# S4 block on one core: block-diagonal first transform of the token tiles, and a new order for the front of the program

## The chip, the cores and the metric

The kernel runs on one core of a Trainium2 chip. A core has five engines with in-order instruction streams: TensorE (PE, matrix products into PSUM banks; its weight loads are listed as PEld), VectorE (DVE), ScalarE (ACT, functions with a scale and a bias, and copies), GpSimd (POOL), and SyncE (SP), which here issues nearly all DMA transfers. The metric is the device time of one execution in microseconds (us), as the median of several runs. For one further execution there is a profile: busy times, the order of instructions, and what each waited for. L412 is line 412 of the kernel.

## The reference

The input `u` has 2048 tokens of 640 channels; a condition vector `c` gives six vectors of 640 values (shift, scale and gate, twice).

```python
mod = (silu(c) @ w_mod).reshape(1, 6, 1, 640)      # sa, ca, ga, sb, cb, gb
h = layernorm(x) * (1 + ca) + sa
x = x + ga * A(h)          # A: for each channel a convolution over all 2048 tokens
h = layernorm(x) * (1 + cb) + sb
x = x + gb * ((silu(h @ w1) * (h @ w3)) @ w2)      # 640 -> 1728 -> 640
```

In `A`, the kernel of the convolution of channel d is `K[d, l] = Re sum_n C[d,n] dt[d] B[d,n] exp(dt[d] A[d,n] l)` with 128 values of n, and the product of the spectra (`rfft`, `irfft`) computes the causal convolution; a skip term `h * Dskip` is added. All is float32.

## The kernel before

**Stages.** The convolution runs as small DFT products on PE in two steps, 32 by 64 (NA = 32, NB = 64). The token tiles are j = 0 to 15, each of 128 tokens. The *front* (0 to 163.5 us) loads and prepares all that is needed: it makes polar forms and logarithms of the parameters (`polar`), the modulation vectors, the normalized tiles (`ln1_norm`), the first transform of each tile (`u_stage1`), and for steps s = 0, 1, 2, ... of 16 channels the tables of exponentials and trigonometric values (`exps`, and the parts named PH, AB, CO, SI, E1, E2, A1, A2), from which PE sums the convolution kernels (kg, pt, uk). Then *rounds* follow, one chapter of 128 channels per 54.7 us, in an order that a table writes out (ROUND): second transforms (`stage2`, L571), product of spectra, inverse transforms, and the tables of later steps. The feed-forward network follows from about 410 us to the end.

**What sets the order.** The program is written as calls in sequence. A scheduler may move instructions on PE, DVE, POOL and SP as far as dependencies and buffers let it, but the helpers `act` (L135) and `acopy` (L138) keep all of ACT's instructions in the order in which they are written. PSUM tiles are named by tags (Z, A, B, pb, pk); a tag with one buffer means that a new user waits until the last one has been read.

**Modulation.** Columns of `w_mod` are multiplied by silu(c), spread over four column groups of the array of 32 each. `mod_sums` (L305) gives the blocks k = 0 to 3 to the four groups and block 4 to group 0 again; a one-column matmul (L316 or L358) adds the four groups up. `mod_early` fills `cols`, five of its passes before the first tiles; `mod_cols` makes later ones from weights that `w_load` (L206) brings, near the end of the front. `mod_shift` (L322 to L341) divides shift by scale: the result r is wanted as a row (`pr`, then `rrow`) and, weighted by the column sums of the DFT matrix (c1), as a shift to be added to the transform (`rc`, `ps`, `shift`).

**First transform.** `u_stage1(j)` makes for the four 32-token blocks of a tile the real and imaginary part of a 32-point DFT. Eight matmuls (L412) use 32 rows and 64 columns of the array each, so that eight of them fit beside each other; `pu[0]` (tag Z) takes blocks 0 and 1, `pu[1]` (tag A or B by turns) blocks 2 and 3. For even j four 1-row matmuls (L404) put the shift into `pu[0]` ahead of them, and ACT copies `pu[0]` (L138). For odd j DVE adds the shift while it evacuates `pu[0]` (L417). DVE evacuates `pu[1]` for all j (L418). One DMA of 640 KB (L419) then stores the tile's result to `us` in DRAM; chapters read it back with `u_load` (L557).

**The loop of the front.** For tk = 0, 1, 2, ... the loop makes the tables of step tk + 2, the kernels of earlier steps, the tiles 2 tk + 4 and 2 tk + 5 (the first four stand ahead of the loop), the loads of later x tiles (`ln1_load`, L374, seven buffers) and the normalization of the pair tk + 3 (DVE statistics L383 and L384, POOL L385 and L386, DVE L387, then two ACT instructions x<-x,rs on L135). At tk = 4 to 8 `w_load` is issued, at 5 to 8 `mod_cols(tk - 5)`, at 7 the eight loads of `u_load` for chapter 0, and `mod_cols(4)` stands ahead of the first rounds.

Of the kernel before, what the change touches and what calls it, by code (L numbers as in the profile page):

```python
# [9 lines left out]
F32 = mybir.dt.float32  # L10
# [7 lines left out]
P = 128  # L18
# [19 lines left out]
def consts():  # L38
# [34 lines left out]
    c1 = s1r.reshape(4, NA, 2 * NA).sum(axis=1, keepdims=True).repeat(NA, axis=1).reshape(P, 2 * NA)  # L73
# [5 lines left out]
    misc = np.concatenate([selx, stepx, s1r, c1, one4, toq, tog], axis=1)  # L79
    f = lambda v: np.ascontiguousarray(v, dtype=np.float32)  # L80
    return {"s1": f(s1), "s2": f(s2), "i1": f(i1), "i2": f(i2), "iota": iota, "misc": f(misc),
# [26 lines left out]
def tile_kernel(ctx: ExitStack, tc: tile.TileContext, a):  # L108
# [4 lines left out]
    us = dram.tile([2, 2, NA, NB, D // 2], F32, name="us")  # L113
# [70 lines left out]
    rrow = pm_.tile([P, D], F32, name="rrow")  # L184
    shift = pm_.tile([P, D // 2], F32, name="shift")
    cols = pm_.tile([P, 7, KD], F32, name="cols")
    lt = pm_.tile([P, 2, D - DC], F32, name="lt")
    misc = pm_.tile([P, 9 * NA + 1 + P], F32, name="misc")
    selx, stepx = misc[:, :NA], misc[:, NA:4 * NA]
    s1r, c1, one4 = misc[:, 4 * NA:6 * NA], misc[:, 6 * NA:8 * NA], misc[:, 8 * NA:8 * NA + 1]  # L190
    toq, tog = misc[:, 8 * NA + 1:8 * NA + 1 + P], misc[:, 8 * NA + 1 + P:]
# [7 lines left out]
    l2 = flat[2][:, 4 * D:4 * D + 2 * (D - DC)]  # L199

# [27 lines left out]
    prma = a["prm"].rearrange("i n d -> n i d")  # L228
    nc.sync.dma_start(cT, a["c"])
# [9 lines left out]
    def polar(cs, E):  # L239

        are, aim, br, bi, cr, ci = (prm[:, i, cs] for i in range(6))
        ld, dtc, m, t, g_r, g_i = (v[:, cs] for v in (ldt, dt, m0, t3, gr, gi))
        k0, nk = cs.start // P, (cs.stop - cs.start) // P

        E.tensor_tensor(g_r, br, cr, op=OP.mult)
        E.tensor_tensor(m, bi, ci, op=OP.mult)
        E.tensor_tensor(g_r, g_r, m, op=OP.subtract)
        V.tensor_tensor(g_i, br, ci, op=OP.mult)
        V.tensor_tensor(t, bi, cr, op=OP.mult)
        V.tensor_tensor(g_i, g_i, t, op=OP.add)  # L250
        q, q2, ag, ai = br, bi, cr, ci
        act(q, g_r, AF.Square)
        act(q2, g_i, AF.Square)
        act(ag, g_r, AF.Abs)
        act(ai, g_i, AF.Abs)
        yield
        V.scalar_tensor_tensor(q, q, 1e-36, q2, op0=OP.max, op1=OP.add)
        act(q, q, AF.Ln)

        V.tensor_tensor(m, ag, ai, op=OP.subtract)  # L260
        V.scalar_tensor_tensor(t, ag, 1e-30, ai, op0=OP.max, op1=OP.add)
        V.reciprocal(q2, t)
        V.tensor_tensor(m, m, q2, op=OP.mult)
        act_set("trig_and_small")
        act(m, m, AF.Arctan)
        act(ag, g_r, AF.Sign, scale=-1.0)
        act(ai, g_i, AF.Sign, scale=-1.0, bias=tiny)

        V.scalar_tensor_tensor(aim, aim, 0.25 / math.pi, dtc, op0=OP.mult, op1=OP.mult)
        magic = 12582912.0  # L270
        V.tensor_scalar(t, aim, magic, None, op0=OP.add)
        V.tensor_scalar(t, t, -magic, None, op0=OP.add)
        V.tensor_tensor(aim, aim, t, op=OP.subtract)
        V.tensor_scalar(thi[:, cs], aim, TURN, 2147483520.0, op0=OP.mult, op1=OP.min)
        yield

        nt = 2 * nk
        nat = lambda v: v.rearrange("n (t p r j) -> n t r p j", t=nt, p=4, r=2)
        rows = lambda v: v[:, :nk * P].rearrange("n (t r p j) -> n t r p j", t=nt, p=4, r=2)
        for k in range(nt):  # L280
            E.tensor_tensor(rows(lt[:, 0])[:, k], nat(are)[:, k], nat(dtc)[:, k], op=OP.mult)
        for k in range(nt):
            V.tensor_tensor(rows(lt[:, 1])[:, k], nat(q)[:, k], nat(ld)[:, k], op=OP.add)
        for i, dst in enumerate((la, lm)):
            raw = lt[:, i, :nk * P].rearrange("n (b c) -> n b c", c=32)
            both = l2[:, :2 * nk * P].rearrange("n (b s c) -> n b s c", s=2, c=32)
            acopy(both.bitcast(F32R)[:, :, 0], raw)
            V.tensor_tensor(both[:, :, 1], raw, both[:, :, 0], op=OP.subtract)
            pT = psS.tile([P, 2, 512], F32, name="pT", tag="AB"[i], bufs=1).rearrange("p a b -> p (a b)")
            for k in range(nt):  # L290
                PE.transpose(pT[:, k * P:(k + 1) * P], l2[:, k * P:(k + 1) * P], ident)
            acopy(dst[:, 2 * k0:2 * k0 + nt], pT[:, :nt * P].rearrange("p (k n) -> p k n", k=nt))

        V.tensor_scalar(m, m, 0.5 / math.pi, 0.125, op0=OP.mult, op1=OP.add)
        V.tensor_tensor(m, m, ag, op=OP.mult)
        V.scalar_tensor_tensor(m, m, 0.25, ai, op0=OP.add, op1=OP.mult)
        V.tensor_scalar(phi[:, cs], m, TURN, 2147483520.0, op0=OP.mult, op1=OP.min)  # L297


    def mod_sums(w, pm):  # L300

        n = w.shape[2]
        for k in range(KD):
            g = slice(k % 4 * NA, k % 4 * NA + NA)
            PE.matmul(pm[g, :n], scb[:, k], w[:, k, :], start=(k < 4), stop=(k > 0), tile_position=(0, g.start))  # L305
# [13 lines left out]
    def mod_shift():  # L319
# [9 lines left out]
        for k in range(KD):  # L329
            PE.matmul(pr[:64, k * P:(k + 1) * P], r[:, k:k + 1].broadcast_to([P, 64]), ident, start=True, stop=True)  # L330
        V.tensor_copy(rrow[:64], pr[:64, :D])
        rc = pm_.tile([P, WC], F32, name="part", bufs=2)[:, :KD * 2 * NA].rearrange("p (k c) -> p k c", k=KD)
        V.tensor_tensor(rc, bc(c1, 1, KD), bc(r, 2, 2 * NA), op=OP.mult)
        ps = psS.tile([P, 512], F32, name="ps", tag="pk", bufs=1)
        for k in range(KD):
            for hh in range(2):
                lo, hi = max(k * P, hh * 320), min(k * P + P, hh * 320 + 320)
                if lo < hi:
                    PE.matmul(ps[hh * 64:hh * 64 + 64, lo - hh * 320:hi - hh * 320], rc[:, k],
                              ident[:, lo - k * P:hi - k * P], start=True, stop=True, tile_position=(0, hh * 64))  # L340
        V.tensor_copy(shift, ps[:, :320])  # L341
# [50 lines left out]
    usw = us.rearrange("h c f b d -> (h c f) b d")  # L392
    usr = us.rearrange("h c f b d -> h c b f d")

    def u_stage1(j):
# [3 lines left out]
        u = hpz.tile([P, 4, D // 2], F32, name="u", bufs=2)  # L399
        pu = [psS.tile([P, 2, 512], F32, name="pu", tag=t, bufs=1) for t in ("Z", "AB"[j % 2])]  # L400
        one = j % 2 == 0
        for q in range(2 if one else 0):
            for hh in range(2):
                PE.matmul(pu[0][hh * 64:hh * 64 + 64, q, :320], c1[q * NA:q * NA + 1],  # L404
                          rrow[q * NA:q * NA + 1, hh * 320:hh * 320 + 320],
                          start=True, stop=False, tile_position=(q * NA, hh * 64))
# [1123 lines left out]
```

## Time and profile before

| | |
|---|---|
| median of 3 runs | 968.77 us (967.21 to 969.94) |
| profiled execution | 975.08 us, its span 973.3 us |
| front | 0 to 163.5 us |
| rounds, then the rest of the convolution | 163.5 to about 410 us |
| feed-forward network | about 410 to 973.3 us |
| PE busy over the span | 896.1 us (92%) |
| DVE, ACT, POOL busy | 714.1, 543.0, 282.4 us |

In a row of a timeline stand the start and the length in us, the engine, the line, the operation, output<-inputs by the program's names, sizes, and how many instructions (x) the row joins; in brackets the idle time of the engine before it and what ended that. `PE 32*64 32x320 f32` is a matmul that uses 32 rows and 64 columns of the array and streams 320 columns; a float32 product leaves two records. Tiles that share memory by turns are named after the memory's first user: `uk` or `A` may be a weight block or a parameter. In a row of windows stand the stretch, its length, each engine's busy time with the number of instructions, the clock granted to PE (1.00 is full), the busy share of the DMA engines and GB/s. A row of waits has total, times and longest.

### The profile page before, as it was taken

How to read it: one execution, taken by the hardware profiler on the slowest of the kernel's cores; microseconds unless marked ns; L12 is line 12 of the kernel's file. 1: busy time of each engine (PE TensorE's matmuls, PEld its weight loads, DVE VectorE, ACT ScalarE, POOL GpSimd, SP SyncE). 2: the span in 40 equal slices, each digit the busy share in tenths (PEclk: the TensorE clock that was granted, in tenths of full speed). 3: DMA queues.
4: the chain of work that ended last, by engine and by line, in shares of the span. 5: the costliest groups of instructions: out<-in, count | busy, mean ns of one | idle time of the engine just before them, and what ended most of it. 6: DMA issues, size and time to landing. Idle time of an engine off the chain costs nothing.

```text
span 973.3 us, 20145 instructions
## 1 busy us (share of the span) xinstructions
PE 896.1 (92%) x7984; PEld 675.4 (69%) x7984; DVE 714.1 (73%) x1259; ACT 543.0 (56%) x795; POOL 282.4 (29%) x278
## 2 busy tenths in 40 slices
PE   4978787889888899899999999999999999999998
PEld 2534444666666666567888888777888888888886
DVE  5598865999999996767666665677786766654675
ACT  4568675999999984236433333455743333333332
POOL 1372343455455641113422220121252222200000
PEclk8555777999999999899999999999999999999999
DMA  9463576655665688785213112895422221113443
GB/s 267 143 228 131 198 202 179 163 147 140 170 162 145 171 224 245 220 216 194 91 55 108 55 55 78 234 272 187 146 84 64 77 66 53 54 41 94 149 150 122
DMA packets 103571, 140.73 MB, mean 145 GB/s; under 512 B 20564, under 2 KB 62676, under 8 KB 103476
## 3 DMA queue, kind: packets, MB, share of 16 engines
q1 hardware_dynamic: 99668, 129.34, 46.0%
q0 software_dynamic: 2304, 7.74, 2.4%
q10 hardware_dynamic: 1504, 2.36, 0.8%
q8 instruction: 63, 1.03, 0.4%
q14 instruction: 32, 0.26, 0.1%
HBM read 107.94 MB, written 31.46 MB: 143 GB/s over the span
## 4 chain that ended last, share of the span: by engine, by line
PE 76%; ACT 9%; DVE 7%; DMA 4%; issue 3%; POOL 0%; ACTq 0%; SPq 0%; DVEq 0%; POOLq 0%
PE ps L102 55%; PE p L571 6%; ACT A L135 3%; PE pz L613 3%; PE pk L522 2%; PE pt L540 2%; ACT cs L135 2%; DMA zs<-zt 2%; PE pq L445 2%; PE pa L435 1%; PE pm L305 1%; PE pu L412 1%; ACT uk L138 1%; DMA uk<-in_w_mod_dram 1%; PE pm L316 1%
## 5 line engine op out<-in xcount | busy, mean ns | idle before, releaser
L102 DVE TENSOR_TENSOR s<-ps,s 128x512 f32<-128x512 f32 x138 | 94.9, 688 | 80.4 <-PE ps L102 79.5
L473 POOL TENSOR_TENSOR ph<-thi,iota 128x1024 int32<-128x1024 int32 x40 | 91.9, 2298 | 154.4 <-DVE A L505 54.0
L102 DVE TENSOR_TENSOR gl<-rw,gh 128x640 fp32r<-128x640 f32 x87 | 78.2, 899 | 65.2 <-ACT gh L102 65.1
L102 ACT CAST gh<-rw 128x640 fp32r<-128x640 f32 x87 | 63.3, 727 | 104.2 <-PE ps L102 63.4
L571 PE MATMUL p<-uk,s 128*64 128x256 f32 x640 | 79.4, 390 | 14.0 <-ACT uk L138 5.8
L102 PE MATMUL ps<-xA,gh 128*128 128x512 f32 x280 | 87.8, 392 | 0.4 <-ACT xA L102 0.4
L102 PE MATMUL ps<-gh,uh 128*128 128x512 f32 x224 | 87.5, 391 | 0.0
L102 PE MATMUL ps<-gl,uh 128*128 128x512 f32 x224 | 87.2, 389 | 0.0
L102 POOL TENSOR_TENSOR S<-rw 128x256 f32<-128x256 f32 x46 | 36.8, 801 | 170.7 <-DVE S0l L102 160.0
L102 PE MATMUL ps<-gh,ul 128*128 128x512 f32 x208 | 81.1, 390 | 0.0
L571 PEld LDWEIGHTS p<-uk,s 128*64 128x64 f32 x640 | 45.9, 139 | 37.8 <-issue 9.7
L498 DVE TENSOR_TENSOR E<-A,cs 128x1024 f32<-128x1024 f32 x40 | 60.4, 1511 | 3.2 <-ACT cs L135 2.5
L102 PEld LDWEIGHTS ps<-xA,gh 128*128 128x128 f32 x280 | 52.1, 188 | 13.0 <-ACT xA L102 0.9
L102 PE MATMUL ps<-xA,gl 128*128 128x512 f32 x140 | 54.6, 390 | 0.0
L474 POOL TENSOR_TENSOR ph<-ph,phi 128x512 int32<-128x512 int32 x40 | 48.5, 1213 | 5.0 <-DVE phi L297 2.0
L540 PE MATMUL pt<-s,K 128*64 128x128 f32 x640 | 48.3, 291 | 1.4 <-ACT uk L138 1.4
L505 DVE TENSOR_TENSOR A<-A,ph 128x1024 f32<-128x1024 f32 x40 | 48.9, 1223 | 0.0
L102 ACT ACTIVATE s<-ps 128x512 f32<-128x512 f32 (+1 forms) x33 | 19.7, 597 | 51.3 <-PE ps L102 51.3
L102 PEld LDWEIGHTS ps<-gl,uh 128*128 128x128 f32 x224 | 42.0, 188 | 9.0
L102 PEld LDWEIGHTS ps<-gh,uh 128*128 128x128 f32 x224 | 42.0, 188 | 8.7
L522 PE MATMUL pk<-E 128*32 128x64 f32 x1280 | 45.9, 233 | 1.5 <-issue 0.9
L613 PE MATMUL pz<-Y,i 64*128 64x128 f32 x640 | 44.4, 282 | 2.8 <-issue 2.7
(255 smaller groups left out, 2270.4 us busy)
## 6 DMA issues: line engine op xcount, KB each, us to landing
rw<-in_w_dram SPq DMA_DIRECT2D x52, 320.0 KB
us<-u SPq DMA_DIRECT2D x16, 640.0 KB
s<-in_s_dram SPq DMA_DIRECT2D x40, 256.0 KB
i<-in_i_dram SPq DMA_DIRECT2D x40, 256.0 KB
rw<-in_wg_dram SPq DMA_DIRECT2D x31, 320.0 KB
rw<-in_wu_dram SPq DMA_DIRECT2D x28, 320.0 KB
uk<-us SPq DMA_DIRECT2D x32, 256.0 KB
zs<-zt SPq DMA_DIRECT2D x32, 256.0 KB
```

The lines of the kernel that those rows point to most:

```text
L102: ins = fn(*args, **kw)
L135: return tc.keep_in_program_order(S.activation(*args, **kw))
L138: return tc.keep_in_program_order(S.copy(out, in_))
L445: keep(PE.matmul(pQ[s][:, rr, :256], w[r, t, :], bc(sel[r, js], 2, NA) if i else r1[r, js, :], start=(i == 0), stop=(i == 1), tile_positio ...
L473: hold(G.tensor_tensor(p, bc(thi[:, sl], 2, NPH), bc(iota, 1, SD), op=OP.mult))
L474: keep(G.tensor_tensor(p[:, :, :NA], p[:, :, :NA], bc(phi[:, sl], 2, NA), op=OP.add))
L498: keep(V.tensor_tensor(EC[s][:, :, 1:3, :], AA[s][:, :, 1:3, :], mid(cs[s]), op=OP.mult))
L505: keep(V.tensor_tensor(A[:, :, 1:3, :], A[:, :, 1:3, :], mid(ph[s]), op=OP.mult))
L522: keep(PE.matmul(pk[dq * 32:dq * 32 + 32, g, :], x[:, g * 4 + dq, 1, :], x[:, g * 4 + dq, 0:3:2, :], start=(st == 0), stop=(st == 1), tile ...
L540: keep(PE.matmul(pt[c * 64:c * 64 + 64, g, :], kk[:, g, :], s1[:, c, :], start=True, stop=True, tile_position=(0, c * 64)))
L571: keep(PE.matmul(p2[par * 64:par * 64 + 64, pi, c, :], s2[:, pi * 2 + par, c * 64:c * 64 + 64], uk[:, 0:kn + 1:kn, f, :], start=True, stop ...
L613: ins = keep(PE.matmul(pz[:, par, (g % 2) * 2 + pi, :], i1[r, pi, c, :], Y[r, pi, c, :], start=(c == 0), stop=(c == 1), tile_position=(par ...
```

## The change

**First transform.** The matrix `s1b` holds two 32-point blocks on a block diagonal, so that one matmul on 64 rows and 128 columns makes two token blocks. For each tile there are two matmuls (320 columns each) on rows 64 to 127 into `pu[1]`, and two on rows 0 to 63 into `pu[0]`, ahead of which two 1-row matmuls (L418 of the new kernel) put the shift into `pu[0]`, now for all j. ACT copies `pu[0]` for every tile (L143), DVE adds the shift to `pu[1]` (L427). Each tile is stored with two DMAs of 64 partitions (L429). `us` has the layout [2, 32, 64, 640], and `u_load` has two DMAs per call in every chapter.

**Modulation.** In `mod_sums` block 4 is cut in four pieces, one for each column group. In `mod_shift` the row is spread to all 128 partitions, and one ACT instruction with a scale per partition makes `shift`; `rrow`, `rc` and `ps` leave.

**Order of the front.** The constants that r2 and r1 need are a table of their own (`selstep`), loaded first, and both products are built at once. `polar` becomes a class whose parts are called apart: `log` and `rows` (la, lm) and `exps(0)` stand ahead of `angle` (arctangent) and the modulation. The trigonometric values of step 0, its tables, and those of step 1 stand ahead of or among the first tiles; `exps(2)` comes later. The second of the three gate columns' sums uses tag Z.

```diff
-    us = dram.tile([2, 2, NA, NB, D // 2], F32, name="us")
+    us = dram.tile([2, NA, NB, D], F32, name="us")
...
+        last = [slice(g * n // 4, (g + 1) * n // 4) for g in range(4)]
+        for g in range(4):
+            r = slice(g * NA, g * NA + NA)
+            PE.matmul(pm[r, :n], scb[:, g], w[:, g, :], start=True, stop=False, tile_position=(0, r.start))
+        for g, c in enumerate(last):
+            r = slice(g * NA, g * NA + NA)
+            PE.matmul(pm[r, c], scb[:, 4], w[:, 4, c], start=False, stop=True, tile_position=(0, r.start))
...
-            PE.matmul(pr[:64, k * P:(k + 1) * P], r[:, k:k + 1].broadcast_to([P, 64]), ident, start=True, stop=True)
-        V.tensor_copy(rrow[:64], pr[:64, :D])
...
-        V.tensor_copy(shift, ps[:, :320])
+            PE.matmul(pr[:, k * P:(k + 1) * P], r[:, k:k + 1].broadcast_to([P, P]), ident, start=True, stop=True)
+        act(shift, pr[:, :D], AF.Copy, scale=c1c)
...
+        for hh in range(2):
+            PE.matmul(pu[0][:, hh, :320], c1[:1], shift[:1, hh * 320:hh * 320 + 320], start=True, stop=False,
+                      tile_position=(0, 0))
+        for t in (1, 0):
+            r = slice(t * 64, t * 64 + 64)
             for hh in range(2):
+                PE.matmul(pu[t][:, hh, :320], s1b[r], x[r, hh * 320:hh * 320 + 320], start=(t == 1), stop=True,
+                          tile_position=(r.start, 0))
+        split = lambda v: v.rearrange("p (h d) -> p h d", h=2)
+        acopy(split(u[:, 0]), pu[0][:, :, :320])
+        V.tensor_tensor(split(u[:, 1]), pu[1][:, :, :320], split(shift), op=OP.add)
+        for i in range(2):
+            nc.sync.dma_start(usw[i, :, j], u[i * 64:i * 64 + 64])
...
+        for c in range(2):
+            nc.sync.dma_start(uk[c * 64:c * 64 + 64, 0, fs], usr[c, :, fs, ch * DC:ch * DC + DC])
...
+    V.tensor_tensor(r2, bc(selx, 2, NB), bc(stepx[:, :NB], 1, NA), op=OP.mult)
...
+    first = Polar(d0, V, l2f)
+    first.factors()
+    first.log()
+    first.rows()
+    exps(0)
+    first.angle()
+    first.phase()
...
-    mod_shift()
-    act_set("natural_log_exp_and_others")
-    exps(0)
-    ln1_norm(0)
-    exps(2)
-    ln1_norm(1)
-    do("PH", 1)
-    do("PH", 2)
     for n in ("AB", "CO", "SI"):
         do(n, 0)
+    do("PH", 1)
+    mod_shift()
+    ln1_norm(0)
+    for n in ("E1", "E2", "A1", "A2"):
+        do(n, 0)
+    for n in ("AB", "CO", "SI"):
+        do(n, 1)
+    do("PH", 2)
     u_stage1(0)
     u_stage1(1)
+    do("kg", 0)
+    ln1_norm(1)
+    act_set("natural_log_exp_and_others")
+    exps(2)
+    for n in ("E1", "E2", "A1", "A2"):
+        do(n, 1)
     ln1_norm(2)
```

Three places of the new order. The first is ACT in the front's loop, before: copies of a tile's `pu[0]` (u<-pu), normalizations (x<-x,rs, a pair of tiles), the parameters of the later channels (uk<-uk) and the trigonometric passes (cs, ph).

```order
L138 COPY u<-pu 128x640
L135 ACTIVATE x<-x,rs_539 128x640 x2
L135 ACTIVATE uk<-uk 128x512 x4
L135 ACTIVATE cs<-ph 128x1024
L135 ACTIVATE cs<-cs,hp 128x1024
L135 ACTIVATE ph<-ph 128x1024
L138 COPY u<-pu 128x640
L135 ACTIVATE x<-x,rs_647 128x640 x2
```

The same place now:

```order
L143 COPY u<-pu 128x640 x2
L140 ACTIVATE x<-x,rs_574 128x640 x2
L140 ACTIVATE uk<-uk 128x512 x4
L140 ACTIVATE cs<-ph 128x1024
L140 ACTIVATE cs<-cs,hp 128x1024
L140 ACTIVATE ph<-ph 128x1024
L143 COPY u<-pu 128x640 x2
L140 ACTIVATE x<-x,rs_638 128x640 x2
```

The copies of a pair's two tiles now stand next to each other, where there was one copy.

The second place is PE at a pair of tiles, before (with buffer numbers, so that tiles can be told apart; x_166 and x_168 are two token tiles, misc the constants, pm the modulation):

```order
L412 MATMUL pu_477<-x_168,misc_107 64x320 x3
L404 MATMUL pu_458<-rrow_103,misc_107 64x320
L316 MATMUL pm_441<-misc_107,part_447 128x1
L404 MATMUL pu_458<-rrow_103,misc_107 64x320 x3
L412 MATMUL pu_458<-x_166,misc_107 64x320 x4
L412 MATMUL pu_477<-x_168,misc_107 64x320
```

PE at a pair of tiles now (pu_523 and pu_543 are the two tag Z banks' users of tiles in succession, pu_524 and pu_544 their other halves):

```order
L423 MATMUL pu_510<-x_211,misc_106 128x320 x2
L423 MATMUL pu_524<-x_213,misc_106 128x320 x2
L418 MATMUL pu_523<-shift_103,misc_106 128x320 x2
L423 MATMUL pu_523<-x_213,misc_106 128x320 x2
L423 MATMUL pu_544<-x_295,misc_106 128x320 x2
L418 MATMUL pu_543<-shift_103,misc_106 128x320 x2
L423 MATMUL pu_543<-x_295,misc_106 128x320 x2
```

The small matmuls of two tiles, mixed before, now stand tile after tile in groups of two, the half for `pu[1]` first.

The third place is SP in the first part of the front's loop, before: stores (us<-u) and loads of x tiles.

```order
L419 DMA us<-u 128x1280 x2
L374 DMA x<-in_x_dram 128x640 x2
L419 DMA us<-u 128x1280 x2
L374 DMA x<-in_x_dram 128x640 x2
L419 DMA us<-u 128x1280 x2
L374 DMA x<-in_x_dram 128x640 x3
```

SP there now:

```order
L390 DMA x<-in_x_dram 128x640 x3
L758 DMA uk<-in_prm_dram 128x6x512
L429 DMA us<-u 64x2x640 x12
L390 DMA x<-in_x_dram 128x640 x7
L429 DMA us<-u 64x2x640 x4
L390 DMA x<-in_x_dram 128x640 x2
```

The twelve stores of tiles 0 to 5 now stand ahead of the load of x tile 7, with the loads of seven tiles behind them.

More of the change, by code (lines that the diff above doesn't have):

```diff
@@ L71, in consts @@
     stepx = np.concatenate([np.arange(NB), 64 * np.arange(NA)])[None].repeat(P, 0)
-    c1 = s1r.reshape(4, NA, 2 * NA).sum(axis=1, keepdims=True).repeat(NA, axis=1).reshape(P, 2 * NA)
+    s1b = np.zeros((4, NA, 2, 2 * NA))
+    for q in range(4):
+        s1b[q, :, q % 2] = s1r[q * NA:(q + 1) * NA]
+    s1b = s1b.reshape(P, P)
+    c1 = np.tile(s1r[:NA].sum(axis=0), 2)
     one4 = (np.arange(P) % NA == 0).astype(np.float32)[:, None]
@@ L199, in tile_kernel @@
     l2 = flat[2][:, 4 * D:4 * D + 2 * (D - DC)]
+    l2f = [t3[:, DC + 2 * DC * i:DC + 2 * DC * (i + 1)] for i in range(2)]
     def w_load(w, c0):
@@ L236, in tile_kernel @@
         [w_room(1, 0, 256, 1280), w_room(1, 1, 256, 1280), w_room(1, 2, 256, 1280), w_table(), w_table()])]
[L239 to L289, printed above, removed]
-            for k in range(nt):
[L291 to L297, printed above, removed]
@@ L770, in tile_kernel @@
     u_stage1(3)
[L771 removed]
+    rest = Polar(d1, G, [l2, l2])
     fp = None
@@ L798, in tile_kernel @@
             if tk == 2:
-                next(rest)
+                rest.log()
+                rest.angle()
         do("CO", tk + 2)
@@ L816, in tile_kernel @@
         if tk == 0:
-            next(rest)
+            rest.factors()
         if tk == 3:
-            next(rest, None)
+            rest.rows()
+            rest.phase()
             wm = []
```

135 lines of the change are left out of this document (76 added, 59 removed).

## The prediction

> **What bounds the kernel now.** I read the slices of the page first, then busy times by stage, then what ScalarE (ACT) waits for in the front. In the slices each digit is a fortieth of the span (24.3 us) in tenths.
>
> ```profile
> span 973.3 us, 20145 instructions
> ...
> ACT  4568675999999984236433333455743333333332
> ...
> PEclk8555777999999999899999999999999999999999
> ```
>
> The first four slices (to about 100 us) have the low granted clock; the change lies there. Then the stages, by windows:
>
> ```profile
> core 0: us, PE busy (x) PEld busy (x) DVE busy (x) ACT busy (x) POOL busy (x), PEclk, DMA share, GB/s
> 0.00:34.00 34.00, 19.23 (x90) 10.47 (x90) 17.83 (x62) 11.30 (x21) 4.09 (x8) 0.74 0.97 293
> ...
> 34.00:125.10 91.10, 75.27 (x810) 40.93 (x810) 78.94 (x146) 65.19 (x80) 43.26 (x43) 0.61 0.43 156
> ...
> 129.00:163.50 34.50, 27.40 (x402) 15.77 (x400) 20.96 (x35) 20.74 (x24) 13.56 (x8) 0.85 0.83 212
> ...
> 190.80:245.60 54.80, 46.96 (x946) 35.17 (x947) 52.12 (x81) 53.13 (x65) 29.48 (x16) 1.00 0.57 152
> 410.00:973.30 563.30, 557.42 (x2650) 450.97 (x2650) 373.91 (x653) 238.35 (x413) 109.44 (x142) 0.99 0.39 115
> ```
>
> From 410 us TensorE (PE) is busy 557.42 of 563.30: untouched. In the rounds ACT is busy 53.13 of 54.80: they cost what ACT costs, and the change adds nothing to ACT there. So only the time at which the rounds begin (163.5) can move. The transform of the sixteen token tiles fills 34 to 129 us. No engine is full there (PE 75, DVE 79, ACT 65 of 91), so the chain between engines counts, and ACT, whose instructions run in written order, joins the chains. What it waits for from 34.00 to 125.10, in total, times, longest:
>
> ```profile
> ACT x L135 <- DVE rs L387: 13.7, 6, 3.3
> ACT u L138 <- PE pu L412: 6.0, 2, 4.2
> ACT A L135 <- PE pq L445: 3.8, 4, 1.8
> ACT la L138 <- PE pT L291: 3.4, 1, 3.4
> ACT lm L138 <- PE pT L291: 1.9, 1, 1.9
> ```
>
> These 28.8 us are a little above the idle time of 91.10 − 65.19 = 25.9 us, since ends overlap. I build the changed front as ACT's busy time plus ACT's waits.
>
> **The change part by part.**
>
> *Start of the chain.* VectorE (DVE) now builds the two products r2 and r1 before the parameters land; today they stand behind them.
>
> ```profile
> 8.43 2.29 DVE L737 TENSOR_TENSOR r<-misc 128x2048 fp32r<-128x2048 f32 x1
> ...
> 15.96 1.21 DVE L741 TENSOR_TENSOR r<-misc 128x1024 fp32r<-128x1024 f32 x1
> ...
> 31.51 0.16 DVE L317 COPY cols<-pm 128x2 f32<-128x2 f32 x1 [1.19 <-PE pm L316]
> ...
> 34.00 1.73 ACT L135 ACTIVATE x<-x,rs 128x640 f32<-128x640 f32 x2 [3.26 <-DVE rs L387]
> ...
> 34.62 2.40 PE L330 MATMUL pr<-ident,cols 128*64 128x128 f32 x10 [2.43 <-DVE cols L326]
> ```
>
> That takes 2.29 + 1.21 = 3.5 us out of the way of the last modulation column (31.67); the shorter fifth block of each sum I put at 0.9 over the five early sums (an estimate, ends 0 and 2). Columns are then ready at 27.3. The small vector operations take 34.62 − 31.67 = 2.95, the row matmuls pr 2.40, the new ACT copy into shift 0.68 (the length of a 640-column copy, below): 33.3. The first normalization, behind that copy on ACT, starts at 33.3 instead of 34.00: −0.7. The products rc, their matmuls ps and two DVE copies leave; they lay beside ACT's work, so I credit nothing.
>
> *Work on ACT.* All sixteen first halves are now evacuated by ACT, eight before.
>
> ```profile
> L138 ACT COPY u<-pu 128x640 f32<-128x640 f32 x8 | 5.5, 684 | 6.1 <-PE pu L412 6.0
> ...
> L418 DVE TENSOR_TENSOR u<-pu,shift 128x640 f32<-128x640 f32 x16 | 13.0, 814 | 4.7 <-PE pu L412 4.2 <-issue 0.5
> ...
> 43.43 1.04 ACT L135 ACTIVATE cs<-ph 128x1024 f32<-128x1024 int32 x1
> ...
> 45.79 1.15 ACT L135 ACTIVATE cs<-cs,hp 128x1024 f32<-128x1024 f32 x1
> 46.84 1.04 ACT L135 ACTIVATE ph<-ph 128x1024 f32<-128x1024 int32 x1
> ```
>
> Eight copies more: 8 × 0.684 = +5.5. The three trigonometric passes of step 0 now run ahead of the start: −(1.04 + 1.15 + 1.04) = −3.2. ACT's work to the end of the last copy is 65.19 + 5.5 − 3.2 = 67.5. DVE loses eight additions (8 × 0.81 = 6.5); it is not what ACT waits for in the long waits on pu, so this is worth nothing by itself.
>
> *The pair wait.* Here lies the largest term. Before, two tiles' evacuations stood apart on ACT, and the eight 32-row matmuls of a tile ran on different parts of the array together. Now the two copies of a pair stand next to each other on ACT, and pu[0] has one buffer (tag Z). Between them PE must run, for the second tile, two 1-row matmuls (L418 after) and two on rows 0 to 63 (L423): four slots in series on the same rows. The slot and the hand-overs:
>
> ```profile
> 79.54 1.34 PE L404 MATMUL pu<-rrow,misc 1*64 1x320 f32 x8
> 80.66 1.29 PE L412 MATMUL pu<-x,misc 32*64 32x320 f32 x8
> ...
> 121.11 0.50 PE L404 MATMUL pu<-rrow,misc 1*64 1x320 f32 x4 [0.15 <-DVE u L417]
> ...
> 121.42 0.45 PE L404 MATMUL pu<-rrow,misc 1*64 1x320 f32 x4
> ...
> 94.68 0.67 ACT L138 COPY u<-pu 128x640 f32<-128x640 f32 x1
> ...
> 95.40 1.59 PE L412 MATMUL pu<-x,misc 32*64 32x320 f32 x16 [0.72 <-ACT u L138]
> ```
>
> A group of eight records lasts 80.66 − 79.54 = 1.12 us at the low clock, and twice 121.42 − 121.11, 0.62, at the high one. PE starts 95.40 − 95.35 = 0.05 after a copy ends; handing back I take as the same. A pair costs 4 × 0.62 + 0.1 = 2.6 us at the high clock, 4 × 1.12 + 0.1 = 4.6 at the low. Which clock?
>
> ```profile
> 91.00:94.00 3.00, 3.00 (x76) 2.83 (x74) 2.85 (x7) 2.99 (x6) 1.00 (x3) 0.50 0.34 107
> 94.00:97.00 3.00, 2.21 (x24) 0.69 (x20) 2.29 (x4) 3.00 (x5) 0.68 (x1) 0.91 0.27 113
> 126.00:129.00 3.00, 3.00 (x28) 1.24 (x28) 2.80 (x4) 2.35 (x3) 0.06 (x1) 0.50 0.54 218
> ```
>
> After three full microseconds at 0.50 the clock is granted at 0.91, though another full stretch stays at 0.50; the average of the front is 0.61. The change gives PE more to stream, so I take 3.2 per pair, nearer the fast end: eight pairs, 25.6 us (ends 20.8 and 36.8). The Trainium skill, "TensorE: Matmul & The Clock Gate", Part 1 (the HAM clock gate), says that full clock is granted after about one busy window of 3.4 us and lost after an idle one; the first two rows agree, the third does not plainly. By that rule alone every pair would be fast, which is the first rival.
>
> *The x loads.* SyncE's (SP) queue now holds the stores of tiles 0 to 5 (twelve) ahead of the load of x tile 7; before, loads and stores alternated.
>
> ```profile
> 53.46 1.34 SPq L374 DMA_DIRECT2D x<-in_x_dram  x2
> ...
> 128.93 0.32 SPq L419 DMA_DIRECT2D us<-u  x1
> ...
> 133.80 1.31 SPq L557 DMA_DIRECT2D uk<-us  x2
> ...
> 139.94 9.72 SPq L557 DMA_DIRECT2D uk<-us  x6
> ```
>
> The normalization of tiles 6 and 7 stands on ACT right behind the copies of tiles 4 and 5. After these come a store's issue 0.32, the load's issue 1.34 / 2 = 0.67, 320 KB at the 293 GB/s of the first window (1.1), and up to the longest wait on rs, 3.3: 5.4 us once (ends 0, where the copy is not last, and 6.6, twice that wait). Later loads come with seven buffers' lead, and DVE has the later statistics ahead of the additions, so I drop the other waits on rs; if half of the 13.7 stayed, +6.8. The waits on pq, la and lm were 9.1; the tables made earlier leave 6 (ends 3 and 9).
>
> *Sum for the front.* 33.3 + 67.5 + 25.6 + 5.4 + 6 = 137.8 for the end of tile 15's evacuation. Today it is 128.90:
>
> ```profile
> 128.08 0.82 DVE L417 TENSOR_TENSOR u<-pu,shift 128x640 f32<-128x640 f32 x1 [0.20 <-PE pu L412]
> ```
>
> That is +8.9.
>
> *Tail.* Today the loads of the first transform's result for chapter 0 go out as two (133.80) and six (139.94 to 149.66), with modulation loads between; all eight now stand together behind the stores. Beginning 4.9 after the last evacuation as today and at 9.72 / 6 = 1.62 each, they end 17.9 after it instead of 20.8: −2.9 (ends 0, where the modulation load's room comes no sooner, and −4.8, where the first two take 1.31). The stores with pieces of 2560 bytes and the loads with 512 in every chapter lie beside other work; in the rounds ACT covers them (53.13 of 54.80), and without that cover the 1.7 us of slack per chapter is the price. The last modulation sums get shorter on PE; ends 0 and −1, taken as 0.
>
> Sum: +8.9 − 2.9 = +6.0. The profiled execution took 975.08 (span 973.3), 6.3 above the median of the runs, 968.77; it becomes 981.1, and the median 968.77 + 6.0 = 974.8.
>
> **The rivals.**
>
> *Faster: PE stays at the high clock and the load of x does not hold.* Eight pairs at 2.6 save 4.8 against my sum, the load 5.4: 6.0 − 10.2 = −4.2, 964.6; with the tables' waits at 3 it is 961.6. For it speak the rise at 94 us and PE's added work, against it the 0.50 at 126 and the average of 0.61. Without the load's wait, the pair decides at 3.2 − 0.6 / 8 = 3.1 us.
>
> *Same: only the clock is better.* Pairs at 2.6, load at 5.4: 6.0 − 4.8 = +1.2, 970.0. Gains of the start and losses of the pairs cancel nearly. This is also the case in which the new order does what it says and its lead is spent before the rounds.
>
> *Slower still: PE stays slow and becomes the bound.* Pairs at 4.6: +11.2, 986.0. PE was busy 75.27 of 91.10; each tile goes from about 1.5 slots to four, sixteen tiles: +40 slots or +25 to +45 us at 0.62 to 1.12. At the low clock that would fill PE, which by the rise at 94 us should itself bring the clock up; hence less likely.
>
> **How the numbers follow.** Forecast 0.44, faster rival 0.28, near-same 0.13, slow PE 0.15. The forecast's own range is 969 to 981 (load 0 to 6.6, tail 0 to −4.8). To leave out no more than 2 in 10, the range takes the near-same case and most of the faster one, and stops short of the slow one: 961 to 985. About 0.3% (2.9 us) is what a measurement of this kernel can tell from no change. The faster rival and a sliver of the forecast give 0.31 for faster; half the near-same case and a little of the forecast 0.12 for same; the rest 0.57 for slower.
>
> **What would show it.** In the profile after, the waits of ACT on pu should come to 20 to 37 us in some eight pieces (right if the second copy of a pair waits 2.6 to 4.6); the wait on rs once at about 5, at tiles 6 and 7; the last u evacuated near 138; and the rounds begin near 169.5, with their period still 54.7. The start is right if the first normalization begins near 33. It is wrong if the waits on pu are short because PE runs at full clock, if the additions on DVE and not the copies end the chain, or if the rounds' period changes.

## The result and the profile after

The changed kernel takes 1026.01 us (median of 4 runs, 1020.05 to 1031.08) against 969.36 us before (4 runs): a ratio of 1.0586, 95% interval 1.0508 to 1.0665. It is 57 us slower; 6 were forecast, and the range ended at 985. The four runs fall in two groups, 1020 to 1021 and 1031 us; the profiled execution, 1030.92 us, is of the second, while the one of before (975.08 us) lies 5.7 us above the median given here, so that differences of a few microseconds between two profiles are read with that in mind.

The page's first lines and slices of the changed kernel (one digit is 25.7 us):

```profile
span 1029.1 us, 20049 instructions
...
ACT  3453635669999999533643333246664333333332
...
PEclk9995556779999999999999999999999999999999
```

ACT's nines, the rounds, begin two slices later than before. Stage by stage (columns as in the windows above); the second window ends at the last copy of a tile, the third where the rounds begin, and the last row is everything after that:

```profile
0.00:34.00 34.00, 18.27 (x116) 10.78 (x116) 16.79 (x60) 11.34 (x22) 4.70 (x7) 1.00 0.91 283
34.00:186.90 152.90, 138.30 (x816) 80.29 (x817) 80.82 (x147) 71.20 (x89) 45.47 (x49) 0.65 0.37 100
186.90:219.30 32.40, 23.96 (x338) 15.86 (x334) 18.13 (x28) 23.75 (x27) 7.62 (x4) 0.82 0.92 226
...
219.27:1029.10 809.83, 769.64 (x6659) 606.35 (x6658) 593.10 (x1014) 442.63 (x668) 216.72 (x219) 1.00 0.46 134
```

The same stretch of before, from its first second transform to the end:

```profile
163.45:973.30 809.85, 771.18 (x6659) 607.04 (x6658) 592.64 (x1014) 442.55 (x668) 220.48 (x219) 0.99 0.47 134
```

The rounds and all that follows take 809.83 and 809.85 us: the whole loss lies in the front. The transform of the tiles there lasts 152.9 us instead of 94.9; PE is busy 138.30 of these (78.22 of 94.9 before). ACT's waits from the first normalization to the last copy, in total, times, longest:

```profile
ACT u L143 <- PE pu L423: 49.9, 10, 8.7
ACT x L140 <- DVE rs L403: 9.8, 2, 9.2
ACT A L140 <- PE pq L455: 9.5, 5, 3.2
ACT la L143 <- PE pT L310: 6.8, 1, 6.8
ACT u L143 <- issue: 2.2, 1, 2.2
ACT lm L143 <- PE pT L310: 1.9, 1, 1.9
```

The wait on pu was 6.0 us before. One pair of tiles on ACT and on PE, and, behind the line of dots, a later pair:

```profile
75.14 0.67 ACT L143 COPY u<-pu 128x640 f32<-128x640 f32 x1
75.87 2.49 PE L418 MATMUL pu<-shift,misc 1*128 1x320 f32 x4 [0.52 <-ACT u L143]
78.29 2.50 PE L423 MATMUL pu<-x,misc 64*128 64x320 f32 x4
80.83 0.69 ACT L143 COPY u<-pu 128x640 f32<-128x640 f32 x1 [5.01 <-PE pu L423]
...
136.50 0.69 ACT L143 COPY u<-pu 128x640 f32<-128x640 f32 x1 [0.69 <-PE pu L423]
...
139.47 1.54 PE L550 MATMUL pt<-s,K 128*64 128x128 f32 x10
140.94 2.50 PE L418 MATMUL pu<-shift,misc 1*128 1x320 f32 x4
143.37 2.50 PE L423 MATMUL pu<-x,misc 64*128 64x320 f32 x4
145.91 0.69 ACT L143 COPY u<-pu 128x640 f32<-128x640 f32 x1 [8.71 <-PE pu L423]
```

In the first pair the copy waits for exactly the four slots in series (a slot is the time of one matmul of 320 columns, two records), 2.42 us for two of them: the low clock. In the second it waits for other matmuls too, of the convolution kernels (pt and others), which stand on PE between the two tiles.

### The profile page after: what moved, and what is told of

It reads as the page before. It is cut to its first block, busy times and chain, and to the rows that moved or that the text cites. A ratio compares the mean times of both kernels' runs of the same rounds, so it can differ in the third digit from the quotient of the medians.

```text
span 1029.1 us, 20049 instructions
## 1 busy us (share of the span) xinstructions
PE 950.1 (92%) x7922; PEld 713.2 (69%) x7922; DVE 708.8 (69%) x1248; ACT 548.9 (53%) x804; POOL 274.5 (27%) x278
## 4 chain that ended last, share of the span: by engine, by line
PE 80%; ACT 8%; DVE 5%; issue 3%; DMA 3%; SPq 0%; ACTq 0%; POOL 0%; DVEq 0%
PE ps L107 52%; PE p L577 6%; PE pu L423 4%; PE pt L550 3%; PE pu L418 3%; PE pk L532 3%; PE pz L619 3%; ACT A L140 2%; ACT cs L140 2%; DMA zs<-zt 2%; PE pa L445 1%; PE pq L455 1%; PE pm L328 1%; DVE E L508 1%; ACT uk L143 1%
## 5 line engine op out<-in xcount | busy, mean ns | idle before, releaser
L107 DVE TENSOR_TENSOR s<-ps,s 128x512 f32<-128x512 f32 x138 | 94.9, 688 | 79.8 <-PE ps L107 78.9
L107 PEld LDWEIGHTS ps<-xA,gh 128*128 128x128 f32 x280 | 52.1, 188 | 13.0 <-ACT xA L107 1.0
L423 PE MATMUL pu<-x,misc 64*128 64x320 f32 x128 | 55.3, 705 | 5.9 <-ACT x L140 4.1
L550 PE MATMUL pt<-s,K 128*64 128x128 f32 x640 | 52.0, 298 | 2.2 <-ACT uk L143 2.2
L484 POOL TENSOR_TENSOR ph<-ph,phi 128x512 int32<-128x512 int32 x40 | 49.2, 1231 | 15.0 <-DVE cols L349 12.2
L532 PE MATMUL pk<-E 128*32 128x64 f32 x1280 | 49.2, 240 | 2.3 <-DVE E L511 2.3
L423 PEld LDWEIGHTS pu<-x,misc 64*128 64x128 f32 x128 | 28.3, 298 | 29.0 <-issue 17.9
L550 PEld LDWEIGHTS pt<-s,K 128*64 128x64 f32 x640 | 39.3, 147 | 13.1 <-issue 7.2
```

The costliest lines, as they stand in the source:

```text
L107: ins = fn(*args, **kw)
L423: PE.matmul(pu[t][:, hh, :320], s1b[r], x[r, hh * 320:hh * 320 + 320], start=(t == 1), stop=True, tile_position=(r.start, 0))
L484: keep(G.tensor_tensor(p[:, :, :NA], p[:, :, :NA], bc(phi[:, sl], 2, NA), op=OP.add))
L532: keep(PE.matmul(pk[dq * 32:dq * 32 + 32, g, :], x[:, g * 4 + dq, 1, :], x[:, g * 4 + dq, 0:3:2, :], start=(st == 0), stop=(st == 1), tile ...
L550: keep(PE.matmul(pt[c * 64:c * 64 + 64, g, :], kk[:, g, :], s1[:, c, :], start=True, stop=True, tile_position=(0, c * 64)))
```

## The experiments

For each run the table gives the start of the first normalization, the end of the last tile's evacuation and the first second transform, all from its one profile, and the median time. From the rounds' beginning to the end every profile has 806 to 813 us, so these three columns tell where a kernel gained or lost, within the few microseconds by which executions of one kernel differ: the run with the shift on 32 rows begins its rounds 7 us before the profile of before, and its median is the same.

| kernel | first normalization | last evacuation | rounds begin | median | ratio to before |
|---|---|---|---|---|---|
| before | 34.0 | 128.9 | 163.5 | 969.4 | 1 |
| after | 38.3 | 186.9 | 219.3 | 1026.0 | 1.0586 (1.0508 to 1.0665) |
| new order, old transform | 38.1 | 139.7 | 171.4 | 983.6 | 1.0140 (1.0102 to 1.0179) |
| old order, new transform | 43.7 | 181.6 | 213.2 | 1024.7 | 1.0559 (1.0512 to 1.0606) |
| all matmuls on 128 rows | 39.2 | 157.6 | 189.8 | 1002.1 | 1.0326 (1.0276 to 1.0376) |
| no 1-row matmuls | 38.1 | 159.5 | 191.1 | 1002.6 | 1.0331 (1.0287 to 1.0375) |
| shift matmuls on 64 rows | 34.3 | 162.1 | 192.9 | 1005.6 | 1.0353 (1.0263 to 1.0444) |
| pair's copies apart | 37.4 | 172.0 | 209.0 | 1021.9 | 1.0521 (1.0461 to 1.0582) |
| x loads early | 38.1 | 177.4 | 210.0 | 1020.4 | 1.0505 (1.0440 to 1.0570) |
| 128 rows, DVE evacuates | 37.1 | 145.5 | 180.8 | 994.2 | 1.0236 (1.0163 to 1.0309) |
| the same, x loads early | 39.0 | 139.8 | 175.7 | 987.4 | 1.0178 (1.0134 to 1.0222) |
| before, shift on 32 rows | 31.7 | 122.5 | 156.5 | 968.9 | 0.9998 (0.9974 to 1.0022) |
| before, fifth block cut | 34.1 | 127.9 | 161.5 | 972.1 | 1.0027 (1.0005 to 1.0049) |
| old order, 128 rows, DVE | 39.2 | 135.8 | 172.7 | 983.4 | 1.0141 (1.0117 to 1.0165) |

**Order and transform apart.** First the changed kernel with the old transform:

```diff
-        for hh in range(2):
-            PE.matmul(pu[0][:, hh, :320], c1[:1], shift[:1, ...], ...)
-        for t in (1, 0):
-            ...
+        for q in range(2 if one else 0): ...      # four 1-row matmuls, even tiles
+        for h in range(2): ...                    # eight matmuls of 32 rows x 64 columns
```

> The changed kernel with the transform of before: 32-row matmuls, two shift forms, one store per tile, and the old shift computation; the new order of the front and the cut fifth modulation block stay. Theory A (the four matmuls in series on the same rows, at the low clock, with one PSUM buffer between two adjacent ACT copies, cost the time): nearly all of the 57 us comes back, 955 to 975 us, and ACT's waits on pu fall from 50 us to under 12. Theory B (the new order costs it: late columns, x loads behind the stores, waits on tables): 1000 us or more.

Measured: 983.6 us. 42 of the 57 us come back; theory A's range is missed by 9 us, theory B is out. The waits on pu are 1.9 us, but a wait of 7.6 that the profile gives to no one stands ahead of one copy. What stays, some 13 us, is the order's, the cut fifth block included:

```profile
34.00:139.70 105.70, 85.46 (x918) 46.50 (x922) 94.93 (x156) 67.83 (x82) 47.04 (x46) 0.64 0.41 145
```

About 4 us of it are lost before the tiles, since the first normalization starts at 38.1 instead of 34.0. DVE is the busiest engine of this stretch, 94.93 of 105.70 us, but it was so before, too (82.54 of 94.90). That the front now waits for DVE is not shown: on the chain of work that ended last, from the first normalization on, PE and DVE have about 39 us each. The opposite kernel has the order of before and the new transform:

```diff
 def mod_shift, u_stage1, u_load, us, s1b, c1, c1c: as in the change
 order of the calls, mod_sums, polar: as before
```

> The kernel before with the new transform, shift computation and layout of us alone; order of the front and modulation sums as before. Theory A: 1010 to 1030 us. Theory B: 975 to 990 us, with at most 25 us of waits on pu.

Measured: 1024.7 us, as theory A has it, 54 us more than before (970.9, measured beside it); with the transform in place, the new order adds no more than 1 or 2 us. Not all of the 54 us is the tiles' work, however. `shift` is now made on ACT, in written order, and in the old order that stands ahead of `exps(0)`, so ACT sits idle where it made the tables of step 0 before, and the first normalization starts at 43.7 instead of 34.0:

```profile
18.52 0.37 ACT L142 CAST lm<-pT 128x256 fp32r<-128x256 f32 x1 [1.30 <-PE pT L294]
36.01 0.80 ACT L139 ACTIVATE shift<-pr,misc 128x640 f32<-128x640 f32 x1 [17.11 <-PE pr L333]
```

From the first normalization to the last evacuation this kernel needs 137.9 us, the changed one 148.6, and before 94.9. The two costs (13 and 54) don't add to 57: both hold a late start, and behind it the slow stage is PE's in both kernels with the new transform.

**The clock.** PE was busy for long without a gap in the changed front and was yet at the low clock:

```profile
104.00:122.00 18.00, 18.00 (x88) 10.18 (x88) 8.00 (x25) 13.65 (x18) 3.80 (x4) 0.50 0.25 65
```

The next run gives every matmul of the transform all 128 rows, filled up with zeros in the constants:

```diff
-                PE.matmul(pu[t][:, hh, :320], s1b[r], x[r, ...], start=(t == 1), stop=True,
-                          tile_position=(r.start, 0))
+                PE.matmul(pu[t][:, hh, :320], s1b[:, t * P:t * P + P], x[:, ...], start=(t == 1), stop=True)
...
-            PE.matmul(pu[0][:, hh, :320], c1[:1], shift[:1, ...], ...)
+            PE.matmul(pu[0][:, hh, :320], c1, shift[:, ...], ...)   # c1 is zero but in row 0
```

> The changed kernel with every matmul of the transform on all 128 rows (zeros in the constant matrices where there was nothing), so six slots in series per tile instead of four that overlap with two. Theory C (the clock stays low because few rows of the array take part, though PE is busy without a gap): granted clock from 34 us to the last evacuation rises from 0.65 to 0.85 or more and a pair waits about 3.7 us; 985 to 1010 us. Theory D (the rows taken part do not matter to the clock): clock stays near 0.65, pairs wait 7.3 us or more, 1045 to 1070 us.

Measured: 1002.1 us, 24 us less than the changed kernel although there is more work in series (rows 64 to 127 no longer run beside the others). Theory C holds. The stretch from 67 us to the last evacuation, in the changed kernel and in this one:

```profile
67.00:186.90 119.90, 106.57 (x632) 61.02 (x631) 54.72 (x102) 54.78 (x70) 23.17 (x26) 0.56 0.41 113
```

```profile
67.00:157.60 90.60, 71.79 (x633) 46.17 (x632) 54.68 (x102) 53.92 (x69) 22.57 (x28) 0.91 0.55 149
```

The granted clock is 0.91 instead of 0.56, although PE is busy for a smaller share (79% instead of 89%). The matmuls by groups in the changed kernel:

```profile
L423 PE MATMUL pu<-x,misc 64*128 64x320 f32 x128 | 55.3, 705 | 5.9 <-ACT x L140 4.1 <-ACT lm L143 1.1 <-ACT la L143 0.7
L418 PE MATMUL pu<-shift,misc 1*128 1x320 f32 x64 | 38.4, 741 | 5.8 <-ACT u L143 5.0 <-ACT shift L140 0.9
```

and in the kernel with 128 rows, with one of its pairs, from ACT's timeline, in a fence of its own:

```profile
L423 PE MATMUL pu<-x,misc 128*128 128x320 f32 x128 | 46.0, 506 | 9.0 <-ACT x L142 7.2 <-ACT lm L145 1.1 <-ACT la L145 0.7
L420 PE MATMUL pu<-shift,misc 128*128 128x320 f32 x64 | 25.5, 522 | 6.5 <-ACT u L145 5.6 <-ACT shift L142 0.9
```

```profile
94.21 0.67 ACT L145 COPY u<-pu 128x640 f32<-128x640 f32 x1
97.39 0.69 ACT L145 COPY u<-pu 128x640 f32<-128x640 f32 x1 [2.51 <-PE pu L423]
```

A record lasts 506 to 522 ns instead of 705 to 741, for the same 320 columns, and this pair waits 2.51 instead of 5.01 us (the eight pairs' second copies 2.51 to 5.60). (3.7 us was expected for a pair; in this one the two matmuls into pu[1] ran ahead, before the first copy.) Between the two stands the run in which only the matmuls for the shift have more rows:

```diff
-            PE.matmul(pu[0][:, hh, :320], c1[:1], shift[:1, hh * 320:hh * 320 + 320], ...)
+            PE.matmul(pu[0][:, hh, :320], c1[:64], shift[:64, hh * 320:hh * 320 + 320], ...)   # zero but in row 0
```

> The changed kernel with its two matmuls per tile for the shift on 64 rows instead of one (63 of them zeros in the constant); everything else, and the number of slots in series, as changed. Theory C1 (the 1-row matmuls hold the clock down): most pairs wait about 2.6 us instead of 5.0, the rounds begin 20 to 35 us earlier than in the changed kernel, 990 to 1010 us. Theory C2 (only matmuls on all rows bring the clock up): pairs still at 5.0 us, 1018 us or more.

```profile
L425 PE MATMUL pu<-x,misc 64*128 64x320 f32 x128 | 50.6, 666 | 9.0 <-ACT x L142 7.2 <-ACT lm L145 1.1 <-ACT la L145 0.7
L420 PE MATMUL pu<-shift,misc 64*128 64x320 f32 x64 | 33.1, 651 | 5.3 <-ACT u L145 4.4 <-ACT shift L142 0.9
```

Measured: 1005.6 us. The rows added to the constant are zeros (those of `shift` that go with them are not), the slots are as many, and 20 us are gone: a part of the low clock hung on the 1-row matmuls. Its front starts 4 us earlier, too (34.3). C1's time is right, its reason only in part, since the records' means fall to 651 and 666 ns, not to 500, and the clock from 67 us on is 0.69: the second copies of the pairs wait 2.71 to 6.04 us, and the waits on pu are 32.6 us in all.

**Slots.** The run without the 1-row matmuls:

```diff
-        for hh in range(2):
-            PE.matmul(pu[0][:, hh, :320], c1[:1], shift[:1, ...], start=True, stop=False, ...)
...
-                          start=(t == 1), stop=True,
+                          start=True, stop=True,
```

> The changed kernel without the two 1-row matmuls per tile; it leaves out the shift in the first half (pu[0]) of each tile. Theory A: a pair's second copy waits 2.6 us at the low clock instead of 5.0, PE loses 16 x 2.43 = 39 us of work: 985 to 1000 us. Theory B: 1015 us or more.

Measured: 1002.6 us, 23 us less; theory A's range is missed by 3 us. The waits on pu fall from 49.9 to 22.8 us. It and the run with 64 rows are near each other, but in different ways. Here the matmuls that are left, on 64 rows, still take 694 ns a record (705 in the changed kernel), and the clock from 70 us to the last evacuation is 0.62: what is gained is work, PE being busy 96.21 us from 34 us to the last evacuation instead of 138.30. With 64 rows nothing is left out, and the clock is better.

**What else stood in the changed front.** The copies of a pair drawn apart on ACT:

```diff
+        if tk < 6:
+            u_stage1(2 * tk + 4)
         do("CO", tk + 2)
         do("SI", tk + 2)
...
-            for j in (2 * tk + 4, 2 * tk + 5):
-                u_stage1(j)
+            u_stage1(2 * tk + 5)
```

> The changed kernel with the first tile of each pair in the loop written ahead of the trigonometric passes, so that about 2.2 us of other ACT work stands between the two copies in six of the eight pairs. Theory A1 (ACT's wait between adjacent copies is what costs, PE could go faster): 12 to 13 us less, 1010 to 1016 us. Theory A2 (PE itself is the bound, busy 138 of 153 us at the low clock, and the wait is only where it shows): 1020 to 1032 us.

Measured: 1021.9 us, in A2's range. ACT's waits on pu fall to 27.5 us, with 12.6 more that the profile gives to no one, but the time hardly follows, and PE stays busy 126.50 of 138.0 us: the wait on ACT was where the loss showed, PE's slots at the low clock were what it was made of. And the loads of two x tiles put ahead:

```diff
     u_stage1(0)
     u_stage1(1)
+    ln1_load(7)
+    ln1_load(8)
```

> The changed kernel with the loads of x tiles 7 and 8 issued after the stores of tiles 0 and 1, ahead of eight stores. If the wait of 9.2 us on these loads lies on the path: 1014 to 1020 us. If PE takes up the time: 1021 to 1031 us, with waits on pu longer by as much.

Measured: 1020.4 us, between the two ranges, and like the faster group of the changed kernel's own runs. The long wait on rs is gone, so it came from the order of loads and stores, and that on pu is not shorter:

```profile
ACT u L143 <- PE pu L423: 51.0, 11, 8.7
...
ACT x L140 <- DVE rs L403: 1.2, 2, 0.6
```

How much of the 9.2 us lay on the path is left open by this run.

**Is the new transform good with both faults mended?** All 128 rows, no matmuls for the shift, and DVE adding it in both halves, so that ACT copies nothing:

```diff
-        acopy(split(u[:, 0]), pu[0][:, :, :320])
+        V.tensor_tensor(split(u[:, 0]), pu[0][:, :, :320], split(shift), op=OP.add)
```

> The run with all 128 rows, without matmuls for the shift: DVE adds the shift in both halves while it evacuates them, ACT copies nothing; four slots in series per tile. Theory A with C (slots at the high clock and the hand-over to ACT are what is left of the loss): 965 to 985 us. Rival: DVE, with 16 evacuations more (16 x 0.81 = 13 us), becomes what the front waits for: 988 to 1002 us.

Measured: 994.2 us, in the rival's range; its reason is not shown, since DVE is busy 90.62 of 111.50 us from 34 us to the last evacuation, a smaller share than before. ACT waited 26.3 us once for the normalization of tiles 6 and 7, so the loads were put ahead as well (`ln1_load(7)` and `ln1_load(8)` behind `u_stage1(1)`, as above):

> The run with 128 rows and both halves on DVE, with the loads of x tiles 7 and 8 ahead of eight stores as well. That run's ACT waited 26.3 us once for the normalization of tiles 6 and 7. If that wait is on the path there: 968 to 980 us. If the DVE is the bound: 988 to 996 us.

Measured: 987.4 us, between the two ranges, just under the second. DVE is busy 93.02 of the 105.8 us from 34 to the last evacuation, about the share of before (88% and 87%), and the first normalization starts 5 us later than before. The last run has the same transform in the order of before:

```diff
 transform: s1b on 128 rows, no matmuls for the shift, DVE adds it in both halves
 order of the calls, mod_sums, polar, x loads: as before
```

> The kernel before, its order of the front and its modulation sums, with the new transform on all 128 rows, no matmuls for the shift, and DVE adding it in both halves. If the costs of order and transform add: the run with x loads early (987.4) less what the order alone cost with the old transform (983.6 - 970.9 = 12.7): 971 to 978 us. If the transform with four slots in series per tile costs time also at the high clock: 982 us or more. If it gains on the old one there: under 967 us.

```profile
34.00:135.80 101.80, 76.25 (x695) 46.31 (x695) 88.28 (x150) 68.34 (x80) 47.45 (x42) 0.84 0.49 134
```

```profile
34.08 0.80 ACT L139 ACTIVATE shift<-pr,misc 128x640 f32<-128x640 f32 x1 [15.11 <-DMA uk<-in_prm_dram]
...
39.21 1.72 ACT L139 ACTIVATE x<-x,rs 128x640 f32<-128x640 f32 x2
```

Measured: 983.4 us, in the range of the case that four slots in series cost time at the high clock, too. The trace does not bear that reason out. The clock is up (0.84), PE is busy 76 of 102 us, and of the 9.2 us by which the rounds begin later than in the profile of before, 5.2 are lost at the start: ACT again sits idle 15.11 us ahead of `shift`. From the first normalization to the last evacuation the kernel needs 96.6 us, the profile of before 94.9. So this run doesn't tell whether the new transform on 128 rows is slower than the old one; a kernel with the old order and `shift` made elsewhere wasn't run. None of the kernels with the new transform is as fast as before.

**Two pieces of it on the kernel before.** If rows raise the clock, the 1-row matmuls of the old transform (64 of 320 records) might hold it down too:

```diff
-                PE.matmul(pu[0][...], c1[q * NA:q * NA + 1], rrow[q * NA:q * NA + 1, ...], ...)
+                PE.matmul(pu[0][...], c1z[q * NA:q * NA + NA], rrow[q * NA:q * NA + NA, ...], ...)   # zero but in one row
```

> The kernel before with the shift matmuls of even tiles (L404) on 32 rows instead of one, 31 of them zeros in the constant; nothing else. Theory C1 (rows that stream bring the clock up) with PE's waits on the path: granted clock of the front up from 0.61, 3 to 8 us faster, 961 to 967 us. If the 1-row share there is too small (64 of 320 records of the transform) or PE is not what the front waits for: within 2 us of before.

Measured: 968.9 us, a ratio of 0.9998 (0.9974 to 1.0022): no difference. The granted clock from 34 to 125.1 us is 0.65 instead of 0.61. The share is too small, or PE isn't what that front waits for; the run doesn't tell which. The cut of the fifth modulation block alone, as in the change:

```diff
-        for k in range(KD):
-            PE.matmul(pm[g, :n], scb[:, k], w[:, k, :], start=(k < 4), stop=(k > 0), ...)
+        for g in range(4): ...                    # blocks 0 to 3, one per column group
+        for g, c in enumerate(last):
+            PE.matmul(pm[r, c], scb[:, 4], w[:, 4, c], start=False, stop=True, ...)
```

> The kernel before with the fifth block of each modulation sum cut over the four column groups; nothing else of the change. Each wide sum lasts about 1.0 us less at the low clock on PE; at the end of the front three such sums stand in the chain to the first round: 0 to 3 us faster. If it only shifts PE's load and the clock: within 1.5 us of before.

Measured: 972.1 us, 1.0027 (1.0005 to 1.0049): no gain, if anything 0.3% lost.

## Why the prediction was wrong

The direction was right, the size was not: +57 for +6. By the prediction's own sum, from the first normalization to the last copy:

| term | forecast | measured in the profile after |
|---|---|---|
| first normalization starts | 33.3 | 38.31 |
| ACT's work | 67.5 | 68.74 |
| waits on pu | 25.6 | 49.9 + 2.2 |
| wait for x | 5.4 | 9.8 |
| waits on pq, la, lm | 6 | 9.5 + 6.8 + 1.9 |
| end of the last copy | 137.8 | 186.9 |
| from there to the rounds | −2.9 to before | 32.4 against 34.6: −2.2 |

*The pair wait* is the step that failed: eight at 3.2 us was the forecast, 52.1 us in all was measured, 6.5 a pair. The slots were sized right (four at 1.21 and a hand-over are 5.01), but two things were not. First the clock: "the change gives PE more to stream, so I take 3.2 per pair, nearer the fast end". PE did stream more, but on one row and on 64 rows, and seven of eight pairs were at the low clock, four of them with waits of 5.0 to 5.9 us; the run with 128 rows in the same order, at 0.91 instead of 0.56, shows that the few rows are why. The row of before that stayed at 0.50 while PE was busy 3.00 of 3.00 us was the warning: in it most was matmuls on 32 and 64 rows (pu from 126.67, pa behind and ahead), while the stretch of 3.8 us that ended in the rise at 94 us was pk and pt, all on 128 rows. Second, the wait was priced as if PE had nothing else to do between two tiles; in order on PE stood the matmuls of the convolution kernels, and the three others waited 7.26, 8.71 and 8.71.

*The rival that PE stays slow and becomes the bound* was the right mechanism, and it was given 0.15. Its price was wrong by its own words: it named +40 slots and up to +45 us of work for PE, which had been idle for 91.10 − 75.27 = 15.8 us only, so that up to 29 us more was to be expected in that case; it added only 11.2 us of longer pair waits. Measured, PE's busy time for the transform rose from 33.2 + 12.2 to 55.3 + 38.4, by 48 us, though the count of slots was off: the eight matmuls of a tile did not all run together before, but took 2.41 us at the low clock (sixteen records at 88.50), two slots. The argument that a full PE would itself bring the clock up is refuted by the row from 104 to 122 us above.

*The start.* Columns were to be ready at 27.3. DVE did build r2 and r1 early, but the last column came at 30.45 instead of 31.67, since the weights' sums on PE (with pq and pa between them) were waited for, not DVE. Then the five small operations, with DVE's statistics between them as before, took until 34.39, 3.9 us where 2.95 was forecast:

```profile
30.29 0.16 DVE L343 COPY cols<-pm 128x2 f32<-128x2 f32 x1 [0.38 <-PE pm L342]
...
33.26 1.08 DVE L352 TENSOR_TENSOR cols<-cols 128x5 f32<-128x5 f32 x1
...
34.39 2.50 PE L356 MATMUL pr<-ident,cols 128*128 128x128 f32 x10 [4.14 <-DVE cols L352]
```

The first normalization stood behind the shift on ACT, as forecast, and so started at 38.31, 4.3 us later than before; the step counted a gain of 0.7.

*ACT's work* was right within 1.2 us. *The wait for x* came once, at tiles 6 and 7, as forecast, but at 9.2 us it was longer than its upper end of 6.6. *The tail* is right within 0.7 us by luck, two errors that cancel: the eight loads stood together, but began 8.6 us after the last copy (4.9 was forecast) and took 8.20 / 8 = 1.03 each (1.62). *The waits on pq, la and lm* were three times the forecast: they are waits for the same slow PE, and the step looked only at when the tables are made. That the order of the front costs time by itself was in the forecast only through the x loads; with the old transform it costs 13 us, 4 of them at the start. *The rounds* were untouched, as argued: 809.83 and 809.85 us.

The Trainium skill, "TensorE: Matmul & The Clock Gate", Part 1 (the HAM clock gate), says that about 3.4 us of sustained busy time bring the full clock. The runs here do not agree where matmuls use few rows: from 139 to 153 us PE was busy without a gap, with the 1-row slots of two tiles in it, 2.43 us for each two of them, the length of the low clock. With more rows, zeros in the constant, the same number of slots ran faster.

## What to carry to other kernels

At one clock a matmul of 320 columns took the same time here on 1 row and on 64 (2.42 and 2.43 us for two in series, from 75.87 us in the changed kernel), and four small ones side by side were no longer than one (1.12 us for eight records, at 79.54 in the kernel before). So two half-filled ones in series on the same rows cost as much as eight small ones in two groups. Count slots in series at the low clock before counting instructions, add them to PE's busy time, and compare with its idle time, as the least that such a change costs. Where a stage of thin matmuls keeps PE busy and slow, rows of zeros in the constant can be worth trying; before work is moved to an engine with a written order, read what stands behind it there, as behind ACT's `shift`; and where copies on an in-order engine wait on one PSUM buffer, read what else stands on PE between them.

## What had not been expected of the hardware

The granted clock followed the rows that take part, not only the time that PE is busy: mean record lengths for 320 columns were 741 ns (1 row) and 705 ns (64 rows) in the changed kernel, 651 and 666 with the first on 64 rows, 522 and 506 with all on 128 rows, for the same columns per matmul, and rows counted though their constants were zero. Whether it is rows, or rows times columns, these runs don't separate, since all were 128 columns wide.

And the clock column must be read beside durations: in the changed kernel the stretch from 37.7 to 51 us shows 1.00 while matmuls there have the length of the low clock.

```profile
37.70:51.00 13.30, 13.22 (x72) 7.23 (x76) 12.45 (x22) 5.42 (x8) 2.75 (x6) 1.00 0.20 49
```

```profile
45.99 2.50 PE L418 MATMUL pu<-shift,misc 1*128 1x320 f32 x4
```

At 67.49 us, in the same trace, the same four records take 1.34. The view shows 1.00 from the start of the profile until 73 us, so the mean of 0.65 for that front is too high; the comparison with 128 rows above is from 67 us on.
